# Linear attention, routed experts and FFN: Gram products in one row setting, DMA copies in place of the third transpose, other costs for the order's planner

## The chip, the cores and the metric

The kernel runs on one core of one Trainium2 chip. The time is the device time of one execution in microseconds; the profile is of one further execution of the same program.

## What is computed

The reference has three parts, each feeding the next: a delta-rule attention with a state of 48x48 for each of 4 sequences x 8 heads over 768 tokens, a top-1 mixture of eight experts, and a dense FFN with SiLU. Only the first is touched here:

```python
k_n = k / (np.linalg.norm(k, axis=-1, keepdims=True) + 1e-06)
state = np.zeros((B, H, D, D), dtype=np.float32)     # 4, 8, 48, 48
for t in range(S):                                   # 768 tokens
    kt, vt, bt = (k_n[:, :, t], v[:, :, t], beta[:, :, t, None])
    y[:, :, t] = np.einsum('bhd,bhde->bhe', q[:, :, t], state)
    v_old = np.einsum('bhde,bhd->bhe', state, kt)
    state = state + bt[:, :, :, None] * np.einsum('bhd,bhe->bhde', kt, vt - v_old)
```

Behind it, for each of the 3072 tokens, expert = argmax(x @ w_gate), x = gate * relu(x @ w1[expert]) @ w2[expert], and then out = (g @ w_out) with h = x @ w_in and g = h * sigmoid(h).

## The kernel before

Attention is computed in chunks of 128 tokens. A *group* is one chunk of one sequence with its 8 heads (24 groups, named g), and two groups of the same chunk make a *pair* (12 pairs). Within a chunk the recurrence becomes matrix algebra: Gram products of the keys with themselves (L) and of keys with queries (P), an inverse of a triangular matrix by levels of 16, 32 and 64, and a chain that takes the state to the next chunk. Values are kept as two fp16 parts, high and low, whose products are added in PSUM.

Steps of a group, by their names in the planner:

- *front*: the loads lk, lq, lv; norms; the high parts (qh, knh on ScalarE) and low parts (ql on VectorE, knl on GpSimd) go into TMq and TMk, tiles of 128 tokens x 8 heads x 128 columns, in which a head has its high part in one half and its low part in the other. Heads alternate: in TMk an even head has the high part at column 0 and the low one at 64, an odd head the other way round (`part`). duh copies the high parts of k into both halves of TMh with two VectorE instructions. trk, trq and trh turn TMk, TMq and TMh by a DMA transpose each, to TTk, TTq and TTh with the features on partitions 0 to 47 and 64 to 111.
- *Gram* (`grams`): mm0 to mm3 are two heads each. For each head and for L and P there is one matmul over partitions 0 to 111 and one over the 48 partitions of `rows` (at 0 or 64), added in the same PSUM tile `mp` of the pool pm (two buffers). mt masks on VectorE, mh rounds to fp16 on ScalarE, ml takes the rest on GpSimd.
- *levels* and *chain*: xm, Tm, Vm and their copies for each level; then rm, re, rh, z0m, zs, em, ee, zm, zh, zl, ym, ye for the output, and sm, se, sh, sl, sd for the state. scr, lm, st and tv carry diagonal blocks through DRAM.
- *router*: rt, rc, rl, rg and steps of the pair, ending in a scatter of token numbers (ri0, ri1).

The order of all these instructions is a list made beforehand: class `Plan` simulates each engine's queue, with a cost for each step (GROUP and PAIR: name, engine letter, us, what it needs), buffers held (GHELD, PHELD, BUFS), a delay between steps of different engines, and a rank by pair number times EARLY, by the length of the way to the end and by a constant for each step (LATER). D in it is SP's queue, which issues every plain DMA of attention in order, so that a DMA whose source isn't ready holds those behind it. The engines then run their instructions in that order, each waiting by semaphores for what it needs.

After attention, the experts and the FFN run with tiles of 432 and 512 tokens; their code isn't touched.

Of the kernel before, what the change touches and what calls it, by code (L numbers as in the profile page):

```python
# [8 lines left out]
F16 = mybir.dt.float16  # L9
# [19 lines left out]
class Plan:  # L29
# [17 lines left out]

    GHELD = """k lk / sqk kn; q lq / sqq ql; s2 sqk / sqr; s2 sqq / sqq; s2 vq / vq; kn kn / knl; TTk trk / rm mm0 mm1 mm2 mm3; TTq trq / ym mm0 mm1 mm2 mm3; TTh trh / mm0 mm1 mm2 mm3;
# [112 lines left out]
    def order(self):  # L161
# [96 lines left out]
class Attention:  # L258
# [6 lines left out]
    BUFS = dict(k=3, q=3, v=3, ss=2, r0=1, r1=1, w=5, rn=2, s2=1, kn=1, TTk=6, TTq=8, TTh=2, t=3, Mh=8, Ml=8, Lm=2, Ln=1, Tl=2, pr=1, Xl=1, TVl=1, TV=3,  # L265
# [24 lines left out]
    def constants(self):  # L290
# [6 lines left out]
        self.TMh = cp.tile([128, 8, 128], F16, name="TMh")  # L297
# [11 lines left out]
    def setup(self):  # L309
# [5 lines left out]
        def add(name, e, d, need, users, f):  # L315
            l.append((name, e, d, need, users, f))
# [3 lines left out]
        for n, t, u in [("ztq", self.TMq, ["qh", "ql"]), ("zth", self.TMh, ["duh"])] + [(f"zt{i}", t, [(i, "knh"), (i, "knl")]) for i, t in enumerate(self.TMk)]:  # L320
# [85 lines left out]
    def part(self, t, low, swap=False):  # L406

        b = t[:, 0, 0:1]
        step = 192 if low == swap else 64
        return bass.AP(tensor=b.tensor, offset=b.offset + (64 if low != swap else 0), ap=[list(b.ap[0]), [256, 4], [step, 2], [1, 48]])  # L410

    def front(self, pi, g, c, b, a, pr):
# [4 lines left out]
        heads = lambda x: x.rearrange("p (j two) d -> p j two d", two=2)  # L417
# [38 lines left out]
        def qh():  # L456
            nc.scalar.activation(out=self.part(self.TMq, False, True), in_=heads(st["q"]), func=AF.Copy, scale=pr["rn"][:, a, 8:9])

        def ql():
            for h in range(2):  # L460
                hi, lo = self.part(self.TMq, False, True)[:, :, h], self.part(self.TMq, True, True)[:, :, h]
                nc.vector.scalar_tensor_tensor(out=lo, in0=heads(st["q"])[:, :, h], scalar=pr["rn"][:, a, 8:9], in1=hi, op0=ALU.mult, op1=ALU.subtract)

        def knh():
            nc.scalar.activation(out=self.part(TMk, False), in_=heads(st["kn"]), func=AF.Copy)

        def knl():
            nc.gpsimd.tensor_tensor(out=self.part(TMk, True), in0=heads(st["kn"]), in1=self.part(TMk, False), op=ALU.subtract)
# [9 lines left out]
        return [("lk", lambda: load("k", self.k)), ("lq", lambda: load("q", self.q)), ("lv", lambda: load("v", self.v)), ("vs", vs), ("vq", vq), ("sqk", sqk), ("sqr", sqr), ("sqq", sqq), ("kn", kn), ("qh", qh), ("ql", ql), ("knh", knh), ("knl", knl), ("duh", duh), ("trk", lambda: tr("TTk", TMk)), ("trq", lambda: tr("TTq", self.TMq)), ("trh", lambda: tr("TTh", self.TMh))]  # L478
# [236 lines left out]
    def chain(self, pi, g, c, b, a, pr):  # L715
# [654 lines left out]
```

## Time and profile before

| | |
|---|---|
| three runs | 1183.87 us median (1177.86 to 1187.93) |
| profiled execution | 1179.6 us, its span 1177.9 us |
| TensorE busy, share of the span | 1041.7 us, 88% |
| VectorE | 684.2 us, 58% |
| ScalarE | 540.1 us, 46% |
| GpSimd | 367.0 us, 31% |
| mean granted TensorE clock | 0.873 |

Busy time is the time in which an engine executes at least one instruction. Matmuls overlap in TensorE's pipeline, so their durations add up to more than the busy time, and the distance between two starts tells what one of them takes from the engine. The granted clock is a share of 2.4 GHz; 0.50 is 1.2 GHz. DMA share is the mean busy share of the core's 16 DMA engines.

### The profile page before, as it was taken

The numbers are of one execution on the slowest core, as the hardware profiler recorded it, in microseconds if no ns is written. First come the engines' busy times: TensorE is split into PE (matmuls) and PEld (weight loads), VectorE is DVE, ScalarE is ACT, GpSimd is POOL, SyncE is SP. The second block draws the span as 40 slices with busy tenths as digits, with TensorE's granted clock in tenths as the row PEclk, the third lists the DMA queues.
The fourth block names the chain that finished last, engine by engine and source line by source line (L and its number), as shares of the span: only waits on it lengthen the run. The fifth ranks groups of instructions, "written<-read, shape, count | busy, mean of one in ns | idle before, by whom it ended". The sixth has DMA issues, their size and how long they took to land. (4 is left out here: it accounts for less than half of the span.)

```text
span 1177.9 us, 21319 instructions
## 1 busy us (share of the span) xinstructions
PE 1041.7 (88%) x8404; PEld 879.5 (75%) x8405; DVE 684.2 (58%) x1443; ACT 540.1 (46%) x1094; POOL 367.0 (31%) x352
## 2 busy tenths in 40 slices
PE   2659988889888987458999999999999999999995
PEld 1325766666665776357999999899999999999995
DVE  5888887787787774354455556994434343333332
ACT  4536676666665566343444443553323232332322
POOL 4766464465554432255333330000101010010101
PEclk9999765675666577569999999999999999999998
DMA  9676897597765632364444444540000000000000
GB/s 243 138 140 112 158 142 126 108 147 123 119 114 91 118 63 69 99 180 130 131 127 130 129 125 133 181 129 1 28 1 27 1 27 1 1 28 1 28 1 29
DMA packets 244404, 108.18 MB, mean 92 GB/s; under 512 B 188488, under 2 KB 234312, under 8 KB 244296
## 3 DMA queue, kind: packets, MB, share of 16 engines
q1 hardware_dynamic: 239944, 96.58, 38.7%
q0 software_dynamic: 4352, 10.16, 2.8%
q8 instruction: 68, 1.11, 0.4%
q14 instruction: 40, 0.33, 0.1%
HBM read 71.34 MB, written 16.50 MB: 75 GB/s over the span
## 5 line engine op out<-in xcount | busy, mean ns | idle before, releaser
L1106 PE MATMUL po<-w,g 128*128 128x384 f32 x1152 | 218.4, 338 | 0.0
L1106 PE MATMUL pf<-yb,w 128*128 128x512 f32 x864 | 216.6, 395 | 0.9 <-ACT yb L1181 0.5
L1106 PEld LDWEIGHTS po<-w,g 128*128 128x128 f32 x1152 | 204.6, 188 | 9.0 <-ACT g L1196 0.3
L1106 PEld LDWEIGHTS pf<-yb,w 128*128 128x128 f32 x864 | 161.3, 188 | 31.4 <-DVE yb L1182 0.9
L1194 DVE TENSOR_TENSOR sg<-pf,sg 128x512 f32<-128x512 f32 x96 | 66.2, 690 | 171.7 <-ACT sg L1193 171.6
L1223 POOL DMA_INDIRECT out_dram<-ob,idsi x24 | 25.0, 1044 | 440.3 <-DVE ob L1222 434.8
L1193 ACT ACTIVATE sg<-pf 128x512 f32<-128x512 f32 x96 | 57.4, 598 | 194.1 <-PE pf L1106 193.3
L550 POOL TENSOR_TENSOR Ml<-t,Mh 128x512 f16<-128x512 f32 x96 | 113.4, 1189 | 103.6 <-ACT Mh L545 103.4
L1106 PE MATMUL py<-h,w 128*128 128x432 f32 x576 | 127.1, 361 | 3.7 <-ACT yT L1146 3.1
L1106 PE MATMUL ph<-xT,w 128*128 128x432 f32 x576 | 125.4, 363 | 1.0 <-DVE xT L1078 1.0
L1106 PEld LDWEIGHTS ph<-xT,w 128*128 128x128 f32 x576 | 109.8, 191 | 6.6 <-DVE xT L1078 1.3
L1106 PEld LDWEIGHTS py<-h,w 128*128 128x128 f32 x576 | 106.4, 188 | 10.7 <-ACT yT L1146 3.4
L1197 DVE TENSOR_TENSOR g<-sg,g 128x512 fp32r<-128x512 f32 x96 | 66.3, 691 | 55.1 <-PE po L1106 41.9
L540 DVE TENSOR_TENSOR t<-mp,c 128x512 f32<-128x512 f32 x96 | 65.0, 685 | 53.0 <-PE mp L536 50.3
L1196 ACT ACTIVATE g<-sg 128x512 fp32r<-128x512 f32 x96 | 60.6, 631 | 62.6 <-DVE sg L1194 62.6
L1052 DVE TENSOR_TENSOR w<-raw,w 128x768 fp32r<-128x768 f32 (+1 forms) x56 | 61.4, 1106 | 28.5 <-ACT w L1051 28.2
L545 ACT ACTIVATE Mh<-t 128x512 f16<-128x512 f32 x96 | 58.7, 625 | 41.0 <-DVE t L540 40.7
L533 PE MATMUL mp<-TTh,TTk 112*128 112x128 f16 x192 | 52.3, 272 | 27.3 <-DVE t L540 15.5
L1128 ACT ACTIVATE h<-ph 128x432 fp32r<-128x432 f32 x64 | 33.6, 525 | 75.7 <-PE ph L1106 73.8
L1051 ACT ACTIVATE w<-raw 128x768 fp32r<-128x768 f32 (+1 forms) x56 | 51.6, 934 | 32.8 <-DMA raw<-in_moe_w_dram 32.4
L1129 DVE SCALAR_TENSOR_TENSOR h<-ph,h 128x432 fp32r<-128x432 f32 x64 | 38.5, 601 | 47.6 <-ACT h L1128 46.7
L1070 POOL DMA_INDIRECT xrow<-xd,xi x32 | 34.3, 1073 | 89.1 <-issue 82.8
(195 smaller groups left out, 1996.0 us busy)
## 6 DMA issues: line engine op xcount, KB each, us to landing
TV<-scr SPq DMA_DIRECT2D x24, 512.0 KB, 4.4
raw<-in_moe_w_dram SPq DMA_DIRECT2D x24, 512.0 KB, 4.4
raw<-in_moe_w_dram SPq DMA_DIRECT2D x32, 384.0 KB, 3.9
raw<-in_moe_w_in_dram SPq DMA_DIRECT2D x12, 512.0 KB, 4.3
raw<-in_moe_w_out_dram SPq DMA_DIRECT2D x16, 384.0 KB, 3.2
xd<-x SPq DMA_DIRECT2D x12, 392.0 KB, 5.3
k<-in_k_dram SPq DMA_DIRECT2D x24, 192.0 KB, 4.2
q<-in_q_dram SPq DMA_DIRECT2D x24, 192.0 KB, 2.9
```

What stands on the lines that cost most here:

```text
L533: nc.tensor.matmul(L, k[0:112], kh[0:112], start=True, stop=False)
L540: nc.vector.tensor_tensor(out=t, in0=st["mp", i], in1=self.con.mask.to_broadcast([128, 2, 256]), op=ALU.mult)
L545: nc.scalar.activation(out=st["Mh"][:, self.bank(i)], in_=st["t", i], func=AF.Copy)
L550: nc.gpsimd.tensor_tensor(out=st["Ml"][:, self.bank(i)], in0=st["t", i], in1=st["Mh"][:, self.bank(i)], op=ALU.subtract)
L1051: nc.scalar.activation(out=h, in_=x, func=AF.Copy)
L1052: (nc.gpsimd if slow else nc.vector).tensor_tensor(out=l, in0=x, in1=h, op=ALU.subtract)
L1106: self.nc.tensor.matmul(out, a, b, start=first and i == 0, stop=last and i == n - 1)
L1129: nc.vector.scalar_tensor_tensor(out=h[:, 1, 0:W], in0=ph[:, 0:W], scalar=0.0, in1=h[:, 0, 0:W], op0=ALU.max, op1=ALU.subtract)
L1193: nc.scalar.activation(out=gf, in_=ph, func=AF.Sigmoid)
L1194: nc.vector.tensor_tensor(out=gf, in0=ph, in1=gf, op=ALU.mult)
L1196: nc.scalar.activation(out=g[:, 0], in_=gf, func=AF.Copy)
L1197: nc.vector.tensor_tensor(out=g[:, 1], in0=gf, in1=g[:, 0], op=ALU.subtract)
```

## The change

The Gram products get a tile KX for each group (two buffers), with two halves: KX[0] has the high part of k on partitions 0 to 47 and again on 64 to 111, KX[1] has the low part on 0 to 47 and zeros elsewhere. Every Gram matmul then runs over partitions 0 to 111, with KX as the weights and TTk or TTq as the moving operand; the number of matmuls stays at four for each head. KX is filled by three DMA copies from TTk inside SBUF (step kx), which wait for trk. trh, duh, TMh and TTh go. The halves of TMk and TMq no longer alternate between heads, so ql is one instruction instead of two, and mm takes neighbouring heads. The planner's DMA costs, the time that each DMA takes to land (LAND), a factor on every TensorE cost (SLOW instead of COLD before WARM), EARLY and LATER are other ones, and so the order of the instructions of attention is another one. GpSimd clears the KX tiles once at the start.

```diff
-        duh V .34 knh; trk D 1.2 knl; trq D 1.2 ql; trh D 1.2 duh; mm0 P .48 trk trq trh; mm1 P .48 trk trq trh; ...
+        trk D 1.28 knl; trq D 1.28 ql; kx D 1.20 trk; mm0 P .48 kx trq; mm1 P .48 kx trq; mm2 P .48 kx trq; mm3 P .48 kx trq;
...
+    LAND = dict(lk=3.4, lq=2.8, lv=2.7, trk=2.8, trq=2.7, kx=2.2, scr=2., lm=5., st=5., tv=4., rs=4.)
-    EARLY, LOOK = 9.70, 0.00
+    EARLY, LOOK = 14.40, 0.00
...
-    WARM, COLD = 60, 1.8
+    SLOW = 1.4
...
-            return 1.75
-        return (.95 if x[1][:2] == "tr" else 1.4) if e == "D" else self.DELAY[e] + 1.3 if f == "D" else 0 if e == f == "P" else self.DELAY[e]
+            return 3.9
+        return self.LAND.get(x[1], 2.) if e == "D" else self.DELAY[e] + .1 if f == "D" else 0 if e == f == "P" else self.DELAY[e]
...
-            start[x], end[x] = t, t + tasks[x][1] * (self.COLD if e == "P" and t < self.WARM else 1)
+            start[x], end[x] = t, t + tasks[x][1] * (self.SLOW if e == "P" else 1)
...
-        self.TMh = cp.tile([128, 8, 128], F16, name="TMh")
+        self.KX = [cp.tile([128, 2, 8, 128], F16, name=f"KX{i}") for i in range(self.BUFS["KX"])]
...
+        for i, t in enumerate(self.KX):
+            add(f"zk{i}", "G", 1.0, [], [(i, "kx")], zero(t.rearrange("p two u c -> p (two u) c")))
...
+    def part(self, t, low):
+        return t[:, :, 64:112] if low else t[:, :, 0:48]
...
-            for h in range(2):
-                hi, lo = self.part(self.TMq, False, True)[:, :, h], self.part(self.TMq, True, True)[:, :, h]
-                nc.vector.scalar_tensor_tensor(out=lo, in0=heads(st["q"])[:, :, h], scalar=pr["rn"][:, a, 8:9], in1=hi, op0=ALU.mult, op1=ALU.subtract)
+            nc.vector.scalar_tensor_tensor(out=self.part(self.TMq, True), in0=st["q"], scalar=pr["rn"][:, a, 8:9], in1=self.part(self.TMq, False), op0=ALU.mult, op1=ALU.subtract)
...
-        def duh():
-            for r in range(2):
-                nc.vector.tensor_copy(self.TMh[:, :, 64 * r:64 * r + 48].rearrange("p (j two) d -> p j two d", two=2), self.part(TMk, False))
+        def kx():
+            KX, TT = self.KX[g % len(self.KX)], st["TTk"]
+            for o, i, r in ((0, 0, 0), (64, 0, 0), (0, 1, 64)):
+                nc.sync.dma_start(KX[o:o + 48, i], TT[r:r + 48])
...
-        u = 4 * (i // 2) + i % 2
-        return slice(u, u + 3, 2)
+        return slice(2 * i, 2 * i + 2)
...
-                    r = self.rows(u)
-                    k, q, kh = (st[t][:, u] for t in ("TTk", "TTq", "TTh"))
-                    L, P = mp[:, j, 0:128], mp[:, j, 128:256]
-                    nc.tensor.matmul(L, k[0:112], kh[0:112], start=True, stop=False)
-                    nc.tensor.matmul(L, kh[r], k[r], start=False, stop=True)
-                    nc.tensor.matmul(P, kh[0:112], q[0:112], start=True, stop=False)
-                    nc.tensor.matmul(P, k[r], q[r], start=False, stop=True)
+                    for o, t in ((0, "TTk"), (128, "TTq")):
+                        for x in range(2):
+                            nc.tensor.matmul(mp[:, j, o:o + 128], KX[0:112, x, u], st[t][0:112, u], start=x == 0, stop=x == 1)
```

## Rows read from the trace of the kernel before

**Rows 1.** The page: span, and busy time of TensorE over the whole run.

```profile
span 1177.9 us, 21319 instructions
...
PE 1041.7 (88%) x8404; PEld 879.5 (75%) x8405; DVE 684.2 (58%) x1443; ACT 540.1 (46%) x1094; POOL 367.0 (31%) x352
```

**Rows 2.** Table by stretches of time: busy us of each engine, granted clock, DMA share.

```profile
core 0: us, PE busy (x) PEld busy (x) DVE busy (x) ACT busy (x) POOL busy (x), PEclk, DMA share, GB/s
23.00:418.00 395.00, 339.05 (x4123) 239.19 (x4123) 308.88 (x760) 235.96 (x548) 221.24 (x213) 0.73 0.73 125
418.00:487.00 69.00, 55.25 (x1011) 48.06 (x1010) 35.67 (x99) 41.38 (x97) 15.51 (x14) 0.70 0.31 64
```

**Rows 3.** TensorE in order of time: start us, us, line, out<-in, tile, count.

```profile
301.43 0.21 PE L765 MATMUL pc<-Z0h,Ml 128*128 128x48 f16 x1
...
302.03 0.49 PE L766 MATMUL pc<-Z0s,c 128*128 128x384 f16 x1
...
306.48 0.18 PE L792 MATMUL pc<-Zh,TMk 128*48 128x48 f16 x1
...
307.03 0.18 PE L793 MATMUL pc<-Zl,TMk 128*48 128x48 f16 x1
...
310.76 0.23 PE L533 MATMUL mp<-TTh,TTk 112*128 112x128 f16 x1 [0.85 <-DMA TTk<-TMk]
...
312.37 0.23 PE L535 MATMUL mp<-TTq,TTh 112*128 112x128 f16 x1
...
317.43 0.29 PE L533 MATMUL mp<-TTh,TTk 112*128 112x128 f16 x1
...
320.07 0.22 PE L764 MATMUL pc<-Z0h,Mh 128*128 128x48 f16 x1
```

**Rows 4.** Table by stretches, two pieces of Gram matmuls.

```profile
317.43:320.07 2.64, 2.64 (x13) 1.24 (x13) 0.00 (x0) 1.02 (x4) 1.15 (x1) 0.50 0.65 113
310.76:312.37 1.61, 1.61 (x11) 0.95 (x11) 0.52 (x3) 1.20 (x3) 1.55 (x4) 1.00 1.51 163
```

**Rows 5.** Groups by line, shapes apart: busy us, mean ns, idle before and its cause.

```profile
L540 DVE TENSOR_TENSOR t<-mp,c 128x512 f32<-128x512 f32 x96 | 65.0, 685 | 53.0 <-PE mp L536 50.3 <-POOL Ml L550 1.9 <-POOL kn L454 0.5
...
L533 PE MATMUL mp<-TTh,TTk 112*128 112x128 f16 x192 | 52.3, 272 | 27.3 <-DVE t L540 15.5 <-DMA TTk<-TMk 11.8
...
L462 DVE SCALAR_TENSOR_TENSOR TMq<-q,rn,TMq 128x192 f16<-128x192 f32 x48 | 30.9, 682 | 1.0 <-ACT TMq L457 1.0
...
L472 DVE COPY TMh<-TMk 128x384 f16<-128x384 f16 x48 | 23.5, 530 | 3.4 <-DMA TTh<-TMh 2.0 <-ACT TMk L465 1.2
...
L765 PEld LDWEIGHTS <-Ml 128*128 128x128 f16 x192 | 15.4, 115 | 0.0
...
L784 DVE SCALAR_TENSOR_TENSOR Zl<-pz,Zh 128x384 f16<-128x384 f32 x24 | 13.2, 549 | 7.2 <-ACT Zh L780 7.2
```

**Rows 6.** Tiles TMh, TMq, TTh: ns of one instruction (min/median/max), first and last start.

```profile
L472 DVE COPY TMh<-TMk x48: 239/260/1210, 15.0 to 391.3; 128x384 f16<-128x384 f16 x48
...
L462 DVE SCALAR_TENSOR_TENSOR TMq<-q,rn,TMq x48: 399/413/1405, 14.0 to 383.6; 128x192 f16<-128x192 f32 x48
...
L476 SPq DMA_TRANSPOSE TTh<-TMh x24: 1231/1275/4223, 16.5 to 392.4; - x24
```

**Rows 7.** DMA issues: count, KB each, median us from issue to landing.

```profile
TV<-scr SPq DMA_DIRECT2D x24, 512.0 KB, 4.4
...
scrM<-Mh SPq DMA_DIRECT2D x48, 64.0 KB, 2.5
...
TTh<-TMh SPq DMA_TRANSPOSE x24, 3.5
```

**Rows 8.** SP's queue in order of time, one issue of a load.

```profile
318.56 0.53 SPq L426 DMA_DIRECT2D k<-in_k_dram  x1
```

**Rows 9.** Waits from 23 to 418 us: us in total, times, longest us.

```profile
PE mp L533 <- DMA TTk<-TMk: 11.8, 6, 6.3
```

**Rows 10.** Groups by line of GpSimd, shapes apart.

```profile
L318 POOL MEMSET X<- 128x512 f32 x3 | 1.5, 527 | 0.0
```

More of the change, by code (lines that the diff above doesn't have):

```diff
@@ L29 @@
 class Plan:
-    GROUP = """lk D .55; lq D .55; lv D .55; vs G .79 lv; vq A .51 vs; sqk A .41 lk; sqr V .47 sqk; sqq A .51 lq; kn G .79 nrm7 lk; qh A .51 nrm6 lq; ql V .66 qh; knh A .41 kn; knl G .87 knh;
-        duh V .34 knh; trk D 1.2 knl; trq D 1.2 ql; trh D 1.2 duh; mm0 P .48 trk trq trh; mm1 P .48 trk trq trh; mm2 P .48 trk trq trh; mm3 P .48 trk trq trh;
+    GROUP = """lk D .50; lq D .50; lv D .45; vs G .79 lv; vq A .51 vs; sqk A .41 lk; sqr V .47 sqk; sqq A .51 lq; kn G .79 nrm7 lk; qh A .51 nrm6 lq; ql V .5 qh; knh A .41 kn; knl G .87 knh;
+        trk D 1.28 knl; trq D 1.28 ql; kx D 1.20 trk; mm0 P .48 kx trq; mm1 P .48 kx trq; mm2 P .48 kx trq; mm3 P .48 kx trq;
@@ L36 @@
         mt0 V .6 mm0; mt1 V .6 mm1; mt2 V .6 mm2; mt3 V .6 mm3; mh0 A .52 mt0; mh1 A .52 mt1; mh2 A .52 mt2; mh3 A .52 mt3; ml0 G 1.11 mh0; ml1 G 1.11 mh1;
-        ml2 G 1.11 mh2; ml3 G 1.11 mh3; scr D 1.0 mh0 mh1 mh2 mh3; tv D 1.46 st; xm16 P .47 tv mh3; xe16 V .6 xm16; Tm16 P .21 xe16; Te16 A .37 Tm16; Vm16 P .25 xe16;
+        ml2 G 1.11 mh2; ml3 G 1.11 mh3; scr D 1.28 mh0 mh1 mh2 mh3; tv D .37 st; xm16 P .47 tv mh3; xe16 V .6 xm16; Tm16 P .21 xe16; Te16 A .37 Tm16; Vm16 P .25 xe16;
         Ve16 A .48 Vm16 Tm16; xm32 P .25 Te16 Ve16; xe32 A .53 xm32; Tm32 P .2 xe32; Te32 A .27 Tm32; Vm32 P .25 xe32; Ve32 A .53 Vm32 Tm32; xm64 P .25 Te32 Ve32;
@@ L39 @@
         xe64 A .48 xm64; Vm64 P .25 xe64; Ve64 A .48 Vm64; rm P .4 trk; re V .5 rm vu2 vs; rh A .41 re; z0m P .25 rh Ve64; z0h A .37 z0m; zs V .47 z0h; em P .64 zs ml0 ml1 ml2 ml3;
-        ee V .47 em; zm P .38 ee; zh A .37 zm; zl V .47 zh; ym P 1.05 zl; ye A .46 ym ysc; rt P .34 ye; rc A .37 rt; rl P .52 rc; rg A .06 rl; sm P .62 zl;
+        ee V .47 em; zm P .38 ee; zh A .37 zm; zl V .47 zh; ym P 1.05 zl; ye A .46 ym ysc; rt P .45 ye; rc A .37 rt; rl P .75 rc; rg A .06 rl; sm P .62 zl;
         se V .53 sm; sh A .5 se; sl V .53 sh; sd V .27 sl"""
@@ L45 @@
-        rs D 1.12 rg; ra0 V .09 rg; ra1 V .08 ra0; ra2 V .08 ra1; ra3 V .08 ra2; ra4 V .09 ra3; rp P .1 ra4; rb0 V .17 rp; rb1 V .08 rb0; rb2 V .08 rb1; rb3 V .07 rb2;
+        vu0 V .19 vr; vu1 V .08 vu0; vu2 V .14 vu1; ysc V .13 vu0 nrm5; lm D .40 scr; l0p G .5; l0 V .2 lm; l1 V .07 l0 l0p; l20 V .19 l1; l21 V .09 l20; l22 V .17 l21;
+        l23 V .09 l22; l40 V .27 l23; l41 V .2 l40; l42 V .27 l41; l43 V .2 l42; l8a G 1.46 l43; l8b V .6 l8a; l8c G 1.46 l8b; l8d V .6 l8c; lo V .4 l8d; st D 1.50 lo;
@@ L46 @@
+        rs D .38 rg; ra0 V .09 rg; ra1 V .08 ra0; ra2 V .08 ra1; ra3 V .08 ra2; ra4 V .09 ra3; rp P .1 ra4; rb0 V .17 rp; rb1 V .08 rb0; rb2 V .08 rb1; rb3 V .07 rb2;
         ri0 G 1.05 rb3; ri1 G 1.05 ri0"""
-    GHELD = """k lk / sqk kn; q lq / sqq ql; s2 sqk / sqr; s2 sqq / sqq; s2 vq / vq; kn kn / knl; TTk trk / rm mm0 mm1 mm2 mm3; TTq trq / ym mm0 mm1 mm2 mm3; TTh trh / mm0 mm1 mm2 mm3;
+    GHELD = """k lk / sqk kn; q lq / sqq ql; s2 sqk / sqr; s2 sqq / sqq; s2 vq / vq; kn kn / knl; TTk trk / rm mm0 mm1 mm2 mm3; TTq trq / ym mm0 mm1 mm2 mm3; KX kx / mm0 mm1 mm2 mm3;
@@ L55 @@
     BUFS = dict(x=1, xT=2, small=2, pm=2, pi=2, pc=2, pz=1, pr=1, scrM=3)
-    AFTER = dict(qh="trq 1", ql="trq 1", duh="trh 1", xe16="Tm16 1 Vm16 1", xe32="Tm32 1 Vm32 1", xe64="Vm64 1", rm="ee 2", xm16="Vm16 1", xm32="Vm32 1", xm64="Vm64 1")
+    AFTER = dict(qh="trq 1", ql="trq 1", xe16="Tm16 1 Vm16 1", xe32="Tm32 1 Vm32 1", xe64="Vm64 1", rm="ee 2", xm16="Vm16 1", xm32="Vm32 1", xm64="Vm64 1")
     DELAY = dict(P=.12, A=.2, V=.13, G=.14)
+    LAND = dict(lk=3.4, lq=2.8, lv=2.7, trk=2.8, trq=2.7, kx=2.2, scr=2., lm=5., st=5., tv=4., rs=4.)
     START = dict(P=0.5, A=1, V=0.7, G=0.7, D=1.75)
-    EARLY, LOOK = 9.70, 0.00
+    EARLY, LOOK = 14.40, 0.00
     LATER = dict(
-        l42=129, ql=9, ee=-194, l22=198, vp=14, rt=61, Vm16=98, zl=-42, zh=-59, z0m=-172, sl=-5, ml1=4, l40=7, Te32=6, xm16=-121, ra0=-7, z0h=-11,
-        mm2=75, vr=-6, rb1=160, rb3=-149, mh2=-84, xe16=-4, nrm2=2, ym=13, xm32=-49, mm3=10, Tm32=-146, rp=-101, l21=6, em=-44, mt2=-48, mt0=-4,
-        xe32=-9, trk=6, Vm64=-19, knl=-120, bl0=-42, l8c=-30)
-    WARM, COLD = 60, 1.8
+        l42=226, ql=9, ee=-190, l22=198, vp=14, rt=61, Vm16=98, zl=-42, z0m=-172, ml1=4, l40=10, Te32=6, xm16=-111, z0h=-6, mm2=75, vr=-7, rb1=160,
+        rb3=-152, mh2=-84, xe16=-29, nrm2=210, ym=13, xm32=-49, mm3=10, Tm32=-146, rp=-89, l21=6, em=-44, mt2=-48, mt0=-4, xe32=-7, trk=6, Vm64=-19,
+        knl=-120, bl0=-42, l8c=-30, Ve64=-12, zt1=-2, nrs=-81, sh=-3, sm=-90, zx64=59, se=-20, l8b=2, l43=-4, b1=29, b3=-52, zs2=10, lo=-8, l0p=-34,
+        nrm1=15, sd=51, zs0=20, kn=-25, zxo=10, l23=-124, zt7=16, nrm0=-18, Te16=30, l0=7, rb=2, lm=-6, vu1=-23, zk0=-30, b2=-14, nrm7=6)
+    SLOW = 1.4
     def __init__(self, chunks, pairs, bufs, held, scratch, setup):
@@ L104, in __init__ @@
         for s in ("knh", "knl"):
-            for r in ("sm", "trk", "duh"):
+            for r in ("sm", "trk"):
                 after(s, r, held)
@@ L258 @@
 class Attention:
-    BUFS = dict(k=3, q=3, v=3, ss=2, r0=1, r1=1, w=5, rn=2, s2=1, kn=1, TTk=6, TTq=8, TTh=2, t=3, Mh=8, Ml=8, Lm=2, Ln=1, Tl=2, pr=1, Xl=1, TVl=1, TV=3,
+    BUFS = dict(k=3, q=3, v=3, ss=2, r0=1, r1=1, w=5, rn=2, s2=1, kn=1, TTk=6, TTq=8, KX=2, t=3, Mh=8, Ml=8, Lm=2, Ln=1, Tl=2, pr=1, Xl=1, TVl=1, TV=3,
                 Rh=2, Z0h=2, Z0s=2, Zh=2, Zl=2, ysc=2, m1=2, m2=2, vsc=6)
@@ L318, in setup @@
         zero = lambda t: lambda: nc.gpsimd.memset(t.bitcast(F32), 0.0)
-        for n, t, u in [("ztq", self.TMq, ["qh", "ql"]), ("zth", self.TMh, ["duh"])] + [(f"zt{i}", t, [(i, "knh"), (i, "knl")]) for i, t in enumerate(self.TMk)]:
+        for n, t, u in [("ztq", self.TMq, ["qh", "ql"])] + [(f"zt{i}", t, [(i, "knh"), (i, "knl")]) for i, t in enumerate(self.TMk)]:
             add(n, "G", 0.15, [], u, zero(t.rearrange("p u (r c) -> p (u r) c", r=2)[:, :, 48:64]))
+        for i, t in enumerate(self.KX):
+            add(f"zk{i}", "G", 1.0, [], [(i, "kx")], zero(t.rearrange("p two u c -> p (two u) c")))
         for m in (16, 32, 64):
@@ L404, in scale @@
         return [("vp", vp), ("vr", vr), *self.steps("vu", vu)]
[L406 to L410, printed above, removed]
+    def part(self, t, low):
+        return t[:, :, 64:112] if low else t[:, :, 0:48]
     def front(self, pi, g, c, b, a, pr):
@@ L416, in front @@
         TMk = self.TMk[g % self.TMK]
-        heads = lambda x: x.rearrange("p (j two) d -> p j two d", two=2)
         def load(nm, src):
@@ L456, in qh @@
         def qh():
-            nc.scalar.activation(out=self.part(self.TMq, False, True), in_=heads(st["q"]), func=AF.Copy, scale=pr["rn"][:, a, 8:9])
+            nc.scalar.activation(out=self.part(self.TMq, False), in_=st["q"], func=AF.Copy, scale=pr["rn"][:, a, 8:9])
         def ql():
-            for h in range(2):
-                hi, lo = self.part(self.TMq, False, True)[:, :, h], self.part(self.TMq, True, True)[:, :, h]
-                nc.vector.scalar_tensor_tensor(out=lo, in0=heads(st["q"])[:, :, h], scalar=pr["rn"][:, a, 8:9], in1=hi, op0=ALU.mult, op1=ALU.subtract)
+            nc.vector.scalar_tensor_tensor(out=self.part(self.TMq, True), in0=st["q"], scalar=pr["rn"][:, a, 8:9], in1=self.part(self.TMq, False), op0=ALU.mult, op1=ALU.subtract)
         def knh():
-            nc.scalar.activation(out=self.part(TMk, False), in_=heads(st["kn"]), func=AF.Copy)
+            nc.scalar.activation(out=self.part(TMk, False), in_=st["kn"], func=AF.Copy)
         def knl():
-            nc.gpsimd.tensor_tensor(out=self.part(TMk, True), in0=heads(st["kn"]), in1=self.part(TMk, False), op=ALU.subtract)
-        def duh():
-            for r in range(2):
-                nc.vector.tensor_copy(self.TMh[:, :, 64 * r:64 * r + 48].rearrange("p (j two) d -> p j two d", two=2), self.part(TMk, False))
+            nc.gpsimd.tensor_tensor(out=self.part(TMk, True), in0=st["kn"], in1=self.part(TMk, False), op=ALU.subtract)
+        def kx():
+            KX, TT = self.KX[g % len(self.KX)], st["TTk"]
+            for o, i, r in ((0, 0, 0), (64, 0, 0), (0, 1, 64)):
+                nc.sync.dma_start(KX[o:o + 48, i], TT[r:r + 48])
         def tr(tag, src):
@@ L476, in tr @@
             nc.sync.dma_start_transpose(out=st[tag], in_=src.rearrange("p u c -> p (u c)"))
-        return [("lk", lambda: load("k", self.k)), ("lq", lambda: load("q", self.q)), ("lv", lambda: load("v", self.v)), ("vs", vs), ("vq", vq), ("sqk", sqk), ("sqr", sqr), ("sqq", sqq), ("kn", kn), ("qh", qh), ("ql", ql), ("knh", knh), ("knl", knl), ("duh", duh), ("trk", lambda: tr("TTk", TMk)), ("trq", lambda: tr("TTq", self.TMq)), ("trh", lambda: tr("TTh", self.TMh))]
+        return [("lk", lambda: load("k", self.k)), ("lq", lambda: load("q", self.q)), ("lv", lambda: load("v", self.v)), ("vs", vs), ("vq", vq), ("sqk", sqk), ("sqr", sqr), ("sqq", sqq), ("kn", kn), ("qh", qh), ("ql", ql), ("knh", knh), ("knl", knl), ("trk", lambda: tr("TTk", TMk)), ("trq", lambda: tr("TTq", self.TMq)), ("kx", kx)]
     def steps(self, name, fs):
@@ L510, in norms @@
         return [("nrs", nrs), *self.steps("nrm", nrm), ("ysc", ysc)]
-    def rows(self, u):
-        return slice(0, 48) if u % 2 else slice(64, 112)
     def bank(self, i):
-        u = 4 * (i // 2) + i % 2
-        return slice(u, u + 3, 2)
+        return slice(2 * i, 2 * i + 2)
     def grams(self, pi, g, c, b, a, pr):
@@ L789, in sm @@
             for u in range(H):
-                h, l = (TMk[:, u, r:r + 48] for r in ((64, 0) if u % 2 else (0, 64)))
+                h, l = (TMk[:, u, r:r + 48] for r in (0, 64))
                 nc.tensor.matmul(sp[:, u], h, Zh[:, u], start=True, stop=False)
```

3 lines of the change are left out of this document (1 added, 2 removed).

## The prediction

> **What bounds the kernel now.** I read four views. The page gives the span, 1177.9 us, and a TensorE that is busy for 88% of it [rows 1]; the profiled execution took 1179.6 us, so 1.7 us lie around the span, and it stands 0.4% under the median of the three runs. That share is a mean over two stages, so the table by stretches comes next [rows 2]. Attention runs up to 487 us. Its Gram products lie between 23 and 418 us, and in those 395 us TensorE is busy for 339, VectorE for 309, ScalarE for 236, GpSimd for 221, and the DMA engines' share is 0.73. The 69 us behind them (levels, state chain, routing of the last groups) hold no Gram product. The experts and the FFN, behind 487, are touched by no edit. So what the change is worth is decided in the 395 us, where TensorE, 86% busy, is the most loaded engine.
>
> The third view is TensorE's order of time in one piece of that stretch, read by distances between starts [rows 3]. Twelve Gram matmuls from 317.43 to 320.07 start 0.220 us apart; ten from 310.76 to 312.37 start 0.161 us apart. The granted clock was 0.50 in the first piece (1.2 GHz) and 1.00 in the second (2.4 GHz) [rows 4]. Other fp16 matmuls are far closer: 15 steps of 48 columns from 301.43 to 302.03 take 0.040 us each at the lower level, and 22 from 306.48 to 307.03 take 0.025 us each at the upper. At the same time per column, 128 columns need 0.040 x 128/48 = 0.107 us and 0.067 us. The Gram matmuls pay 0.11 and 0.09 us more than that, a surcharge that hardly moves with the clock. They differ from the others in one thing: in the code each product over 112 rows is followed by one over 48 rows, at partition 0 or 64, and back. The others keep to 112 or 128 rows, with a new weight load for each matmul as well. I read the surcharge as the price of changing the row setting.
>
> The fourth view is the groups by line [rows 5], for durations and for who waits: VectorE was idle for 50.3 us of the run before its masking step because the Gram bank was not done, and TensorE was idle for 27.3 us before a Gram bank, 15.5 behind VectorE and 11.8 behind the transpose of TTk.
>
> **The change, part by part.** *Gram products.* Four matmuls per head before and after: 24 groups x 8 heads x 4 = 768. The four Gram lines have 192 matmuls each with means of 270 to 274 ns [rows 5]; between 290 ns at the lower level and 230 at the upper [rows 3], a mean of 272 puts 30% at the upper. Today: 768 x (0.7 x 0.220 + 0.3 x 0.161) = 155 us. With one setting (0 to 112 for every matmul): 768 x (0.7 x 0.107 + 0.3 x 0.067) = 73 us. Removed: 82 us of TensorE, all inside the stretch that it bounds. The ends are 0, if the setting is not the cause, and 82 plus whatever clock is won.
>
> The Trainium skill (TensorE: Matmul & The Clock Gate, Back-to-back issue gap) gives about 81 ns for each 128-column matmul in a stream with weight loads; as an estimate that makes 62 us of the 768 and a saving of 93. No run here shows that figure yet.
>
> *VectorE.* The two copies of duh go: 48 x 0.53 = 25 us by their mean, 48 x 0.26 = 12 by their median, since some of them last up to 1.2 us [rows 6]. ql becomes one instruction in place of two: 48 x 0.68 = 33 us by the mean, 48 x 0.41 = 20 by the median [rows 5, 6], against 24 of the nearest kind (128x384, Zl) at 0.549 = 13 [rows 5]. So 19 to 45 us go; if the long ones wait for another engine, the wait may pass to the next instruction, so I take 30.
>
> *DMA.* trh goes: 24 transposes, landing 3.5 us after issue. kx adds 72 copies inside SBUF of 96 KB each, a kind that the trace lacks. The nearest rows are the 64 KB scrM piece at 2.5 us and the 512 KB TV load at 4.4 [rows 7]; I take 2.5, nearer in size, plus two further issues of 0.5 [rows 8]. The copies cannot start before trk has landed, where trh ran beside it. So from trk's landing to the first Gram matmul there are 3.5 us (up to 5.4) that were zero. Issue time on SP nearly cancels, about 1.3 us out [rows 6] and three times 0.5 in. What does not cancel is that kx waits at the head of SP's queue for trk; behind it stand the loads of k, q and v, the scr pieces, TV and the next pair's transposes, and TensorE's levels wait for TV. Cover: TTk has six buffers and TTq eight, so the front may run ahead, and only 6 of the 24 groups wait on TTk today [rows 9]. The first group has no cover: I charge 4 us once (2 to 5). Without cover in all groups it would be 24 x 3.5 to 5.2.
>
> *GpSimd.* Two clears of KX, 128x1024 fp32 words each, are twice a clear of X at 0.53 us [rows 10], so 2 us at the start in place of 0.2; the loads of the first k, q and v and the norms of the first pair cover them. Uncovered they cost under 2.
>
> *Order.* The planner gets longer DMA landings, a factor of 1.4 on all TensorE times and new ranks (EARLY, LATER), so the instructions of attention are issued in another order. That has no row. Its bounds are the idle time before Gram banks, 27 us to gain or as much to lose; I take 0, as neither sign is in the trace.
>
> **Sum.** In the stretch TensorE keeps 339 - 82 = 257 us busy; with today's 56 idle that is 313. VectorE keeps 309 - 30 = 279; of its 86 idle, 50 are waits for Gram banks. A bank comes now after 8 x 0.220 = 1.76 us, then after 0.86, against 0.685 for the mask, so I let 40 of the 50 go: 279 + 46 = 325. The later of the two, VectorE, sets the stretch: 395 becomes 325. With the 4 us at the start, 1179.6 - 70 + 4 = 1113.6, so 1114 us.
>
> **The rivals.** *VectorE or the transfers take over sooner.* If none of VectorE's waits shrinks, because another thing is late where the Gram bank was, only its own 30 us count: 1179.6 - 30 + 4 = 1154; if half of the 50 go, 1129. For it: VectorE at 78% now, and a DMA share that would rise from 0.73 to 0.73 x 395/325 = 0.89 even with equal work. Against it: the waits named on VectorE are mainly those for Gram banks.
>
> *The clock rises too.* Gram stretches run at 0.50 or 1.00, and the stretch as a whole at 0.73 [rows 2, 4]. With the same columns in less time the engine might be granted 2.4 GHz for most of it. TensorE would then need 257 x 0.73 = 188 us, VectorE with all 50 waits gone 315, and the tail up to 55 x 0.30 = 17 less: 1179.6 - 80 - 17 + 4 = 1087. Against it: with VectorE as the pace, TensorE has more gaps.
>
> *The Gram products don't get faster.* If the surcharge is a weight load of about 0.10 us in series with the columns, whatever the rows, each matmul still needs 0.10 + 0.107 = 0.21 us at the lower level and 0.10 + 0.067 = 0.17 at the upper, close to today's 0.220 and 0.161, which is for it. TensorE then stays at 339 + 56, and the time is 1179.6 + 4 = 1184, or 1164 if VectorE's lighter load shortens waits by 20. Against it: in the 48-column streams loads of 115 ns [rows 5] go with starts 0.040 us apart, so there the load does run beside the matmuls. The Trainium skill speaks for this rival: TensorE: Matmul & The Clock Gate, Part 3 (The mechanism) says that a weight load overlaps a matmul in flight only when the row group differs. By it, one setting forfeits overlap; the trace's 48-column streams, all in one group, disagree.
>
> *Slower: the serial copies are exposed.* If the front does not run ahead, each group's Gram products come 3.5 to 5.2 us later behind trk and kx, with SP's queue held meanwhile. Against the 82/24 = 3.4 us that a group gains, it decides from about 4 us exposed per group; if the gain is spent in waits for the copies, the excess at the upper end is 24 x (5.2 - 3.4) = 43 us: 1223. For it: KX has two buffers only, and SP issues strictly in order. Against it: 18 of 24 groups show no wait for TTk now.
>
> **How the numbers follow.** Forecast (1095 to 1130) 0.50; VectorE or transfers sooner (1130 to 1155) 0.22; the clock too (1075 to 1095) 0.15; no faster Gram (1164 to 1184) 0.07; slower (around 1223) 0.06. The range 1080 to 1155 holds the first two and most of the third, about 0.83. A measurement of this kernel tells about 1% from no change. Faster by over 1% (under 1172): 0.50 + 0.22 + 0.15 + 0.02 of the fourth = 0.89; within 1%: 0.05; slower: 0.06.
>
> **What would show it.** Gram matmuls at about 0.107 or 0.067 us between starts, with all lines at 112 rows; Gram sums in the groups by line well under today's; attention's end near 420 us; VectorE's wait for Gram banks near 10 us; VectorE busier than TensorE in the stretch; a new wait of Gram matmuls on KX in a few groups only. Wrong would be: distances still near 0.2 us, or KX as the longest wait of TensorE, or long idle times of TensorE behind TV with kx ahead of it in SP's queue.

## The result and the profile after

The changed kernel takes 1136.5 us (median of four, 1134.6 to 1139.2) against 1180.9 us for the kernel before, measured beside it: a ratio of 0.962 with a 95% interval of 0.956 to 0.968. That is 44 us; the forecast was 66.

The page of the changed kernel, span and busy times, against [rows 1]:

```profile
span 1133.2 us, 21329 instructions
...
PE 932.6 (82%) x8404; PEld 843.4 (74%) x8405; DVE 671.9 (59%) x1371; ACT 539.0 (48%) x1094; POOL 368.3 (33%) x353
```

TensorE lost 109 us of busy time, the span 45, and VectorE only 12. The number of matmuls is the same (8404). The table by stretches, against [rows 2] (columns as there), for the Gram stretch, the tail of attention, and the hand-over to the experts:

```profile
29.60:365.00 335.40, 225.25 (x3898) 199.95 (x3899) 286.15 (x663) 225.75 (x527) 214.68 (x209) 0.73 0.72 145
365.00:441.00 76.00, 58.98 (x1247) 51.26 (x1243) 43.94 (x120) 47.66 (x111) 17.86 (x16) 0.81 0.33 72
441.00:466.00 25.00, 0.93 (x10) 0.84 (x8) 12.44 (x31) 9.25 (x12) 16.53 (x9) 0.50 0.63 185
```

So the Gram stretch shrank from 395 to 335 us (-60), but it begins 6.6 us later (29.6 against 23) and its tail is 7 us longer (76 against 69); the rest is 1 us longer. The two stretches do not hold the same work as before: 1247 matmuls fall into the tail against 1011, and 120 VectorE instructions against 99, so a part of the 60 us has only moved behind the last Gram product. VectorE is now the busiest engine there, 85%, and TensorE has fallen from 86 to 67%.

TensorE in order of time, one piece at each clock, against [rows 3] (the trace merges two matmuls per row):

```profile
255.47 0.28 PE L529 MATMUL mp<-TTk,KX 112*128 112x128 f16 x2
255.58 0.27 PE L529 MATMUL mp<-TTq,KX 112*128 112x128 f16 x2
...
256.25 0.28 PE L529 MATMUL mp<-TTq,KX 112*128 112x128 f16 x2
...
271.30 0.39 PE L529 MATMUL mp<-TTk,KX 112*128 112x128 f16 x2
...
272.13 0.25 PE L757 MATMUL pc<-Z0h,Mh 128*128 128x48 f16 x1
```

```profile
255.47:256.36 0.89, 0.89 (x22) 0.88 (x18) 0.08 (x1) 0.86 (x4) 0.89 (x2) 1.00 0.09 4
271.30:272.14 0.84, 0.84 (x11) 0.84 (x10) 0.84 (x3) 0.52 (x1) 0.39 (x2) 0.50 0.90 190
```

From 255.47 to 256.25 start 14 matmuls, 0.056 us apart, at a granted clock of 1.00; from 271.30 to 272.13 eight, 0.104 us apart, at 0.50. Before, the distances were 0.161 and 0.220. The groups by line, against [rows 5] (a Gram bank is one PSUM tile `mp`, the products of two heads):

```profile
L529 PE MATMUL mp<-TTk,KX 112*128 112x128 f16 x384 | 67.7, 273 | 47.6 <-DVE t L533 29.2 <-DMA KX<-TTk 18.3
...
L533 DVE TENSOR_TENSOR t<-mp,c 128x512 f32<-128x512 f32 x96 | 64.8, 682 | 17.1 <-PE mp L529 15.4 <-POOL Ml L543 0.8 <-POOL v L446 0.6
```

The mean duration of a Gram matmul, 273 ns, is what it was (272), although each now takes half the time from the engine or less: only the distance of starts shows it (the ends of matmuls are modelled in the profile). VectorE's wait for Gram banks fell from 50.3 to 15.4 us. TensorE's own wait before a bank rose from 27.3 to 47.6, 29.2 of it behind VectorE (15.5 before) and 18.3 behind the copies into KX, where 11.8 had been behind TTk.

TensorE's busy time in Gram matmuls alone (table by stretches of tile `mp`: stretch, busy, clock, DMA) of the kernel before and then of the changed one:

```profile
0.00:490.00 490.00, 161.01 (x768) 0.74 0.69 124
```

```profile
0.00:490.00 490.00, 80.73 (x768) 0.75 0.66 142
```

80 us of TensorE's Gram work went, and 45 us of time came of it. (The other 29 of the 109 us fell on the matmuls that are not Gram products; why those take less is not shown, but the kernel before with one row setting, below, lost as much, from 1041.7 to 933.3 us.) What made the 80, and where the other 35 stayed, is what the experiments are for.

### The profile page after: what moved, and what is told of

Same layout as the page of the kernel before. It is cut to its first block, busy times and chain, and to the rows that moved or that the text cites. A ratio compares the mean times of both kernels' runs of the same rounds, so it can differ in the third digit from the quotient of the medians.

```text
span 1133.2 us, 21329 instructions
## 1 busy us (share of the span) xinstructions
PE 932.6 (82%) x8404; PEld 843.4 (74%) x8405; DVE 671.9 (59%) x1371; ACT 539.0 (48%) x1094; POOL 368.3 (33%) x353
## 5 line engine op out<-in xcount | busy, mean ns | idle before, releaser
L529 PEld LDWEIGHTS <-KX 112*128 112x128 f16 x768 | 67.7, 127 | 52.8 <-issue 32.0
L529 PE MATMUL mp<-TTk,KX 112*128 112x128 f16 x384 | 67.7, 273 | 47.6 <-DVE t L533 29.2
L533 DVE TENSOR_TENSOR t<-mp,c 128x512 f32<-128x512 f32 x96 | 64.8, 682 | 17.1 <-PE mp L529 15.4
L529 PE MATMUL mp<-TTq,KX 112*128 112x128 f16 x384 | 67.5, 276 | 0.0
```

Of the source, the lines that this page charges most:

```text
L529: nc.tensor.matmul(mp[:, j, o:o + 128], KX[0:112, x, u], st[t][0:112, u], start=x == 0, stop=x == 1)
L533: nc.vector.tensor_tensor(out=t, in0=st["mp", i], in1=self.con.mask.to_broadcast([128, 2, 256]), op=ALU.mult)
```

## Experiments

My theory: the row setting brought the gain, and VectorE took over the pace. Rivals: the new order brought it; or the gain is whole but the serial copies take a part back. Every time is a median of 4 to 10 runs, every ratio is to the kernel before on the same chip. The changed kernel was not timed again beside the experiments: its own four runs spread over 4.6 us, and the kernel before took 1178.8 to 1180.9 us in the median in the five sets of runs. So a difference of 1 to 3 us to the changed kernel is no effect, and one of 6 to 8 us is just clear of the spread.

**Two row settings again, all else as changed.**

```diff
-  nc.tensor.matmul(mp[:, j, o:o + 128], KX[0:112, x, u], st[t][0:112, u], start=x == 0, stop=x == 1)
+  n = 48 if x else 112
+  nc.tensor.matmul(mp[:, j, o:o + 128], KX[0:n, x, u], st[t][0:n, u], start=x == 0, stop=x == 1)
```

> The changed kernel, with the second product of each pair taken over 48 rows again (the other rows of KX[1] are zero, so the sums are the same); order, DMA copies and all else stay. If the row setting is what made the Gram products slow, distances between Gram starts go back from 0.107/0.055 us to about 0.22/0.16, TensorE's busy time grows by 80 us or more and the time goes back to 1165 to 1185. If the order or the DMA side brought the gain, the time stays within 1136 to 1150.

This run took 1179.2 us, ratio 0.999 (0.996 to 1.002): the whole gain is gone. Starts are 0.22 us apart again at a granted clock of 0.50 (TensorE in order of time; two matmuls per row), TensorE's busy time is 1035.2 us against 932.6, and Gram matmuls are busy for 164.8 us:

```profile
253.35 0.51 PE L530 MATMUL mp<-TTk,KX 112*128 112x128 f16 x2
253.79 0.51 PE L530 MATMUL mp<-TTq,KX 112*128 112x128 f16 x2
254.23 0.51 PE L530 MATMUL mp<-TTk,KX 112*128 112x128 f16 x2
...
256.84 0.51 PE L530 MATMUL mp<-TTk,KX 112*128 112x128 f16 x2
```

**One row setting in the kernel before.**

```diff
   def rows(self, u):
-      return slice(0, 48) if u % 2 else slice(64, 112)
+      return slice(0, 112)
...
-  nc.tensor.matmul(L, kh[r], k[r], start=False, stop=True)
+  nc.tensor.matmul(L, kh[r], self.none[r], start=False, stop=True)
...
-  nc.tensor.matmul(P, k[r], q[r], start=False, stop=True)
+  nc.tensor.matmul(P, k[r], self.none[r], start=False, stop=True)
```

> The kernel before, with all four Gram products over 112 rows; the two low-part products are taken against a tile of zeros, so those corrections are left out of the result; the third transpose, its copies and the old order stay. If the row setting is the cause, Gram starts are about 0.107 us apart at 1.2 GHz, TensorE's busy time falls by some 80 us and the time to 1130 to 1160 in the old order. If the gain came from the order or the copies, it stays at 1172 to 1190.

This run took 1136.9 us, ratio 0.964 (0.958 to 0.969): the whole gain, with the old order, the third transpose and duh still there. Starts at the upper clock are 0.055 us apart, and Gram matmuls are busy for 77 us:

```profile
251.80 0.22 PE L535 MATMUL mp<-TTh,TTk 112*128 112x128 f16 x1
251.86 0.22 PE L536 MATMUL mp<-none,TTh 112*128 112x128 f16 x1
251.91 0.22 PE L537 MATMUL mp<-TTq,TTh 112*128 112x128 f16 x1
251.97 0.22 PE L538 MATMUL mp<-none,TTk 112*128 112x128 f16 x1
```

**The order alone, both ways.** The changed kernel with the planner's old settings (two of the lines; the old costs, delays and LATER go with them):

```diff
-    EARLY, LOOK = 14.40, 0.00
+    EARLY, LOOK = 9.70, 0.00
...
-    SLOW = 1.4
+    WARM, COLD = 60, 1.8
```

> The changed kernel, ordered with the planner's old costs, delays, EARLY, LATER and start factor (kx at a cost of 1.2 us). If the Gram products bring the gain, 1135 to 1160. If the new order does, 1170 to 1190.

This run took 1133.0 us, ratio 0.961 (0.955 to 0.966), within the spread the same as with the new order. And the kernel before with the new settings (the same lines the other way round, with LAND):

> The kernel before, ordered with the planner's new costs, landings, EARLY, LATER and TensorE factor (trh landing in 2.8 us). If the Gram products bring the gain, 1165 to 1195, either sign. If the new order does, 1136 to 1150.

This run took 1191.7 us, ratio 1.011 (1.007 to 1.014): 1% slower. So the new order brings nothing to the changed kernel that can be measured, and harms the old one a little.

These four settle the cause of the gain: the row setting, and it alone. Three rivals that the list above lacks are answered by the same runs. The zeros in KX are still there in the run with two settings, which is slow. The granted clock is not the cause: at the same mean clock, 0.876, one run of the kernel before with one setting took 1134.1 us, and one of the kernel before itself 1176.1. And it is not the 48 rows by themselves, as far as the trace tells: in the kernel before (TensorE in order of time) a start follows 0.22 us after the one before it whether that was a matmul of 112 rows or one of 48.

```profile
317.43 0.29 PE L533 MATMUL mp<-TTh,TTk 112*128 112x128 f16 x1
317.65 0.29 PE L534 MATMUL mp<-TTk,TTh 48*128 48x128 f16 x1
317.87 0.29 PE L535 MATMUL mp<-TTq,TTh 112*128 112x128 f16 x1
318.10 0.28 PE L536 MATMUL mp<-TTq,TTk 48*128 48x128 f16 x1
```

A stream of 48-row matmuls alone was not run. The next eight runs ask what paces the rest.

**VectorE's load back.**

```diff
+  for r in range(2):        # behind ql
+      nc.vector.tensor_copy(self.TMh[:, :, 64 * r:64 * r + 48], self.part(self.TMq, False))
```

> The changed kernel plus the removed VectorE load: two copies of 128x384 fp16 (as duh had, into an unused tile) behind ql in each group, 48 in all, which wait for nothing new. If VectorE sets the pace of the Gram stretch now, 12 us by their median duration to 25 by their mean come on top of 1136.5: 1148 to 1162. If TensorE or the chain of trk and kx does, under 4 us: 1134 to 1141.

This run took 1142.7 us, ratio 0.969 (0.965 to 0.972), 6 us more for 23 us of copies (17.5 on VectorE's busy time). That lies between the two expectations: VectorE passes on about a third.

**No ml on GpSimd.**

```diff
-  nc.gpsimd.tensor_tensor(out=st["Ml"][:, self.bank(i)], in0=st["t", i], in1=st["Mh"][:, self.bank(i)], op=ALU.subtract)
+  st["Ml"] = self.Mz
```

> The changed kernel without ml on GpSimd (113 us of it); em and ym use a tile of zeros, so the low parts of the Gram products are left out of the result; TensorE's work is the same. If VectorE sets the pace and its overlong instructions are waits for GpSimd, ql's mean falls from 0.84 us to about 0.62 and that of the Ss steps from 1.1 and 0.94 to 0.6 and 0.4, VectorE's busy time by 20 to 35 us and the time to 1100 to 1122. If they wait for something else, means stay and the time is 1128 to 1137.

This run took 1119.0 us, ratio 0.947 (0.943 to 0.950): 17.5 us less, inside what was expected if VectorE sets the pace. VectorE's busy time fell by 41 us, to 631, more than the 20 to 35 expected, though none of its instructions was taken away. Groups by line of VectorE (L798 is sl, which writes the state's low part, L462 and L464 are ql, L801 is sd, which copies the state), the changed kernel first, then this one:

```profile
L798 DVE SCALAR_TENSOR_TENSOR Ss<-Sm,vsc,Ss 48x384 f16<-48x384 f32 x20 | 22.0, 1098 | 0.8 <-ACT Ss L795 0.8
L462 DVE SCALAR_TENSOR_TENSOR TMq<-q,rn,TMq 128x384 f16<-128x384 f32 x24 | 20.1, 839 | 8.9 <-ACT TMq L459 8.7
L801 DVE COPY Ss<-Ss 48x768 f16<-48x768 f16 x20 | 18.8, 942 | 0.6
```

```profile
L464 DVE SCALAR_TENSOR_TENSOR TMq<-q,rn,TMq 128x384 f16<-128x384 f32 x24 | 16.6, 693 | 12.3 <-ACT TMq L461 12.3
L798 DVE SCALAR_TENSOR_TENSOR Ss<-Sm,vsc,Ss 48x384 f16<-48x384 f32 x20 | 16.3, 816 | 0.9 <-ACT x L817 0.6 <-ACT Ss L795 0.3
L801 DVE COPY Ss<-Ss 48x768 f16<-48x768 f16 x20 | 11.6, 580 | 0.6
```

These three hold 16 of the 41 us. Taking work from GpSimd shortened them; that they had stood waiting for GpSimd is the reading that fits, and the last section has one such case. This run also took away GpSimd's own 113 us and TensorE's wait for ml, so it does not tell how the 17.5 us divide.

**sd on ScalarE, and sd left out.**

```diff
-  nc.vector.tensor_copy(Ss[64:112], Ss[0:48])
+  nc.scalar.activation(out=Ss[64:112], in_=Ss[0:48], func=AF.Copy)
```

> The changed kernel with the copy sd (20 of 48x768, mean 0.94 us, median 0.39) on ScalarE instead of VectorE, in the planner too (0.8 us). If VectorE sets the pace: 8 to 19 us less, 1118 to 1129. If not: 1132 to 1140.

This run took 1144.3 us, ratio 0.969 (0.966 to 0.973): slower by 8 us than the changed kernel, outside both expectations. Its order is another one, as the planner sees the move. So I took the copy away with the order untouched (the line above becomes `pass`):

> The changed kernel with the copy sd left out and the planner untouched: the order is the same, VectorE loses 18.8 us of busy time, ScalarE gains nothing, and the state's second copy stays zero, so the low part of k and q against the state is left out of the result. If every engine passes on about 0.4 of what it loses, as the added and removed loads so far did, 1127 to 1131, and the loss with sd on ScalarE lay in the other order. If relief of VectorE by itself brings nothing, 1134 to 1139.

This run took 1135.6 us, ratio 0.964 (0.959 to 0.968). VectorE's busy time fell by 13 us and the time by 1, which is no difference: the second expectation. A theory in which VectorE alone paces falls with this; TensorE's wait for KX grew from 18.3 to 24.9 us instead.

**Half the Gram products**, alone and together with no ml.

```diff
-  for x in range(2):
-      nc.tensor.matmul(..., start=x == 0, stop=x == 1)
+  for x in range(1):
+      nc.tensor.matmul(..., start=True, stop=True)
```

> The changed kernel with only the first of the two products (384 Gram matmuls instead of 768; the low part of k is left out of one side). TensorE loses 384 x 0.055 to 0.107 = 21 to 41 us. If TensorE still sets the pace, 1097 to 1118. If VectorE does, 1128 to 1138.

This run took 1129.6 us, ratio 0.957 (0.953 to 0.960): 7 us for 19 us of TensorE's busy time (31 in the Gram matmuls, 80.7 to 49.3), again about a third. That is not the pace of TensorE; by itself it would fit one of VectorE.

> Both lighter loads in one kernel: half the Gram products and no ml on GpSimd (the low parts left out as in the single runs). Alone they gave 7 and 17.5 us. If TensorE and VectorE with GpSimd are late at different places, the gains add: 1110 to 1114. If they are late at the same places in turn, freeing both gives more than the sum: 1095 to 1107. If a chain of latencies is the floor, less: 1115 to 1120.

This run took 1115.3 us, ratio 0.947 (0.942 to 0.951): 4 us below the run without ml. Of the three expectations it meets the last, a chain of latencies, at its very edge; the sum of the two gains would be 1112, and 3 us do not tell the two apart. That freeing both gives more than the sum is ruled out.

**No copies into KX.**

```diff
   def kx():
-      for o, i, r in ((0, 0, 0), (64, 0, 0), (0, 1, 64)):
-          nc.sync.dma_start(KX[o:o + 48, i], TT[r:r + 48])
+      pass
...
-  nc.tensor.matmul(mp[:, j, o:o + 128], KX[0:112, x, u], st[t][0:112, u], start=x == 0, stop=x == 1)
+  nc.tensor.matmul(mp[:, j, o:o + 128], self.none[0:112] if x else st["TTk"][0:112, u], st[t][0:112, u], start=x == 0, stop=x == 1)
```

> The changed kernel without the 72 copies: the first product takes TTk itself as weights, the second a tile of zeros, both over 112 rows, so TensorE's work and the order are the same and the cross terms of the high and low parts are left out of the result. TensorE waited 18.3 us for KX in the changed kernel. If the chain trk, kx is what takes back a part of the gain, 10 to 18 us less: 1118 to 1127. If the waits only pass to another engine, 1131 to 1138.

This run took 1126.0 us, ratio 0.955 (0.951 to 0.960): 10.5 us less than the changed kernel, near the lower end of the gain expected. The tile view of `mp` of this run (ns of one, min/median/max; first and last start) shows where half of it lies: the first Gram matmul starts at 24.6 us and not at 29.6, the last at 354.6 and not at 364.7.

```profile
L530 PE MATMUL mp<-TTk x192: 216/263/314, 24.6 to 354.5; 112*128 112x128 f16 x192
...
L530 PE MATMUL mp<-TTq,none x192: 218/258/314, 24.9 to 354.6; 112*128 112x128 f16 x192
...
  DVE t L534: 34.3, 16
```

Without the copies TensorE waits longer for VectorE (34.3 us, 16 times, against 29.2, 12 times). The run takes away both the way through trk and kx and the 72 issues on SP's queue (0.58 us each in the median), and does not tell these apart.

> The same and without sd as well (the state's second copy stays zero; order untouched). Leaving out sd alone gave 1 us, and TensorE's wait for KX grew by 6.6 us there. If VectorE's relief was hidden behind the wait for KX, this one gains a further 5 to 13 us on the kernel without the copies: 1108 to 1120. If not, it is within 2 us of it.

This run took 1124.7 us, ratio 0.953 (0.948 to 0.958), 1.3 us below the last and within the 2 us of the second expectation. But the four runs of each spread over 7 to 8 us, so that a gain of 5 without the copies is not ruled out.

The granted clock is a rival for the sizes in these eight runs. From 25 to 350 us it was 0.73 in the trace of the changed kernel, 0.86 without the copies, 0.85 without ml, 0.82 without sd and 0.81 with half the Gram products. It does not set the time by itself: without sd the time stayed, and the four runs of the changed kernel had mean clocks of 0.888, 0.896, 0.890 and 0.918 at 1135.0, 1139.2, 1134.6 and 1138.0 us. What share it has in the 17.5 and 10.5 us is not shown.

## Why the prediction was right or wrong

The direction and the cause of the gain were right, and the time, 1136.5, lies inside the range but outside the likeliest case (1095 to 1130): it is in the range of the rival "VectorE or the transfers take over sooner", though not by its mechanism. That rival let VectorE's waits for Gram banks stay; they fell by 35 us (50.3 to 15.4), where the forecast had 40. The profiled run took 1135.0 us, 21 more than the forecast: 10 of them are the stretch (335 for 325), 7 the tail and 1 the rest, which the sum left as they were, and 2.6 the start (6.6 for 4).

*Gram products: right.* Forecast 155 to 73 us of TensorE; measured 161 to 80.7, a fall of 80 against 82. Starts are 0.104 and 0.056 us apart against 0.107 and 0.067; the upper value, scaled up from 48 columns, came out too high. The prediction's other estimate, 62 us at 81 ns each, was too low. The row setting as the cause is shown from both sides, by taking it out of the changed kernel and by putting it alone into the old one. The rival with the load in series is refuted: it wanted 0.21 and 0.17 us a matmul, and in the piece with starts 0.056 us apart loads are busy for 0.88 of the 0.89 us beside the matmuls, all over one set of rows. The Trainium skill (TensorE: Matmul & The Clock Gate, Part 3, The mechanism) has it that a load overlaps only when the row group differs, and beside it names a background weight buffer as another case; the first rule taken alone disagrees with the traces. The Trainium skill (TensorEngine Tiling (Array Packing), Key Properties) says that a change of tiling mode drains TensorE; the traces agree so far as each change between 112 and 48 rows costs 0.105 to 0.116 us a matmul (0.161 - 0.056 and 0.220 - 0.104), and do not show what happens in that time.

*VectorE's relief: mis-sized.* I took 30 us off VectorE; its busy time fell by 12, below even the lower bound of 19. duh's 23.5 us went and ql fell from 30.9 to 20.1, but other VectorE instructions grew, sl and sd from 14.3 and 14.2 us in the kernel before to 22.0 and 18.8. In the groups by line of the kernel before:

```profile
L805 DVE SCALAR_TENSOR_TENSOR Ss<-Sm,vsc,Ss 48x384 f16<-48x384 f32 x20 | 14.3, 717 | 1.3 <-ACT Ss L802 1.3
L808 DVE COPY Ss<-Ss 48x768 f16<-48x768 f16 x20 | 14.2, 716 | 0.6
```

I had named the passing on of waits and still taken a value in the middle of the range.

*VectorE as the pace: the step that failed.* The sum let the later of two engines set the stretch: 279 + 46 = 325. Measured are 286 busy and 49 idle, 335. That the arithmetic came so close is partly luck, as some 230 matmuls moved from the stretch into the tail, and its reading was wrong: less VectorE work gives 1 us (sd), more costs 6 (duh), and less TensorE work still gives 7. No single engine explains all of these runs. That freed time moves to the next engine in the fixed order is the reading that fits (TensorE's wait for KX grew by 6.6 us without sd, that for VectorE by 5.1 without the copies); of single loads on TensorE or VectorE nothing to two fifths reaches the end. The forecast had let 70 of 82 us through.

*The serial copies: mis-sized.* I charged 4 us at the first group and cover for the rest, and took 2.5 us for a copy to land. They landed after 3.3 us in the median (the page of the changed kernel):

```profile
KX<-TTk SPq DMA_DIRECT2D x72, 96.0 KB, 3.3
```

The first Gram matmul starts 6 us later than before, and without the copies the kernel is 10.5 us faster, 5 of it at the start and as much later. Gram products waited for KX ten times, where I had expected a few groups. The reason I gave against this, 18 of 24 groups without a wait for TTk, was read from a trace in which TensorE was itself late. (The bound of 5.4 us per group was also carried on as 5.2; with 5.4 the slowest case is 1228 us and not 1223.)

*The order: right at zero* for the time of the changed kernel; not for the kernel before, by 1%. But it moved work into the tail, which the sum had left out: attention ends at 441 us and not near 420.

*Clock: not as in the rival.* The Gram stretch was granted 0.73 in the profiled run, as before; the tail 0.81 against 0.70.

The longer tail goes with the new order: with one row setting in the old order, behind the last Gram product at 368.4 us, it holds 1012 matmuls again, as before, and not 1247. What stays open is what paces the stretch now, why sd on ScalarE costs 8 us, and how the 17.5 us without ml divide between VectorE's waits and GpSimd's own work.

## What to carry to other kernels

Read a matmul's cost from the distance of its start to the next, compare it with other shapes per column, and look for a changing row setting where it is too long: padding the 48-row products, which alternated with products of 112 rows, to 112 rows with zeros made every Gram matmul take half the time at the lower clock and a third at the upper. When work is taken from an engine that is 86% busy in an order written out in advance, don't count on the whole of it; here a little over half of the 80 us reached the end, and the reading that fits is that engines that are busy for 64 to 85% of the stretch took turns in being late. Count a DMA that is made dependent on another in full at the first group, where nothing hides it, and do not take its cover elsewhere from a trace in which the engine that waits for it was slower: here the copies cost 5 us at the start and as much again later.

## What the runs showed of the hardware that was not expected

A VectorE instruction with two inputs in SBUF took six times its median while GpSimd ran four instructions in a row. In order of time, of the changed kernel:

```profile
150.32 0.84 POOL L456 TENSOR_TENSOR kn<-k,rn 128x384 f32<-128x384 f32 x1
150.59 3.66 DVE L798 SCALAR_TENSOR_TENSOR Ss<-Sm,vsc,Ss 48x384 f16<-48x384 f32 x1
151.10 1.62 POOL L446 TENSOR_TENSOR v<-v,root 128x384 f32<-128x384 f32 x2
...
152.68 1.15 POOL L543 TENSOR_TENSOR Ml<-t,Mh 128x512 f16<-128x512 f32 x1
```

GpSimd runs four instructions back to back until 153.83; the VectorE one, 0.60 us in the median, began at 150.59 and ended at 154.25. Its whole length is counted as busy, so if it stood waiting, VectorE's 85% holds time of waiting. The Trainium skill (GPSIMD Engine Reference, Specifications) says that the two share SBUF interfaces and contend when VectorE reads two SBUF inputs or runs in a two-port performance mode; the traces agree for two inputs, as sl's mean fell from 1098 to 816 ns and ql's from 839 to 693 without ml. The copy sd has one input and fell too, from 942 to 580; no trace shows its mode. In all, 41 us of VectorE's busy time went with 113 us of GpSimd's work.
